# Attention over grouped heads: 24 output buffers instead of 8, stores issued 30 steps behind instead of 14

## The chip, the cores and the metric

The kernel runs on one core of a Trainium2 chip. The metric is the device time of one execution in microseconds (us); the time shown is the median of several runs. A profile is one more execution, taken by the hardware profiler; its span runs from the first to the last instruction on the core. The engines are named as in the profile: PE (matmul; PEld is its weight load), DVE (VectorE), ACT (ScalarE), POOL (GpSimd) and SP (SyncE, which here issues every DMA).

## The reference

Softmax attention with grouped heads: 16 batches, 32 query heads, 8 key/value heads, 16 queries, 2048 keys, head size 128, all bf16.

```python
B, Hq, Hkv, Sq, Sk, D = 16, 32, 8, 16, 2048, 128

def reference(q, k, v):
    rep = Hq // Hkv
    k = jnp.repeat(k, rep, axis=1)
    v = jnp.repeat(v, rep, axis=1)
    scores = jnp.einsum("bhqd,bhkd->bhqk", q, k) * D ** -0.5
    p = _softmax(scores, axis=-1)
    return jnp.einsum("bhqk,bhkd->bhqd", p, v)
```

Four query heads share one key/value head, so a key/value head has 64 query rows. K and V are 67 MB each and are read once; the output is 2.1 MB.

## The kernel before

The work is cut into 64 pairs of key/value heads (`NP = 64`). The two heads of a pair fill 128 partitions with their query rows. For each pair p there is a chain: K is transposed on DVE (`kt`, L351), PE makes the scores (`S`, L300 and L256), DVE scales them, copies them out and finds the maximum (L373), ACT takes the exponential (`exp`, L413), PE transposes the result (`PT`, L312), ACT copies that out (L423), PE multiplies it with V (`PV`, L330 for most pairs, L336 for the others), and the product is scaled and written as bf16 to an output buffer `Osb` (the norm): on ACT (L436 or L440) for pairs 0 to 58, on DVE (L394) for the last `NLATE = 5`. The order of work on PE and ACT is laid down in two lists, `pe_prog` and `act_prog`; PV and norm of a pair come four pairs (`PVLAG`) behind its exponential.

K comes in loads of 2 MB for two pairs, into `NK = 3` buffers; V in loads of 1 MB, one pair each, into `NV = 7` buffers (the last one in two parts, L221); q in eight loads of 256 KB. The output of a pair is a store of 32 KB: 128 rows of 256 bytes.

All of these are issued by SP, on one queue and in the order of one loop over steps t (L238 to L247). A step may have a load of q, then the load of K for pairs t and t+1 (even t), the load of V for pair t-6 (`VLAG`), and the store of pair t-14 (`SLAG`). Each waits first for what it needs:

- `load_k` (L208) for the transposes that free its buffer,
- `load_v` (L216, L221) for the PV that frees its buffer, that of seven pairs before,
- `store` (L236) for the norm of its pair: `sem_nm` from ACT, `sem_nl` from DVE for the last five.

While SP waits, or while an issue does not go through, nothing that stands behind it on SP is issued. After the loop SP waits for the semaphores of all output buffers (L249), and that ends the kernel.

An output buffer is pair p modulo `NO`. Each has a semaphore, `sem_o`, that its store raises by 16 when it has landed. The norm of pair p waits until the store of pair p - `NO` has landed (L432 on ACT from pair `NO` on, L392 on DVE). The PV of the next pair waits for a norm too (`sem_nm`, L322), because most pairs share one accumulator in PSUM.

Of the kernel before, what the change touches and what calls it, by code (L numbers as in the profile page):

```python
# [13 lines left out]
NKT = 2  # L14
NS = 3
NPT = 4
NO = 8
NQ = 2
NSTAGE = 3
VLAG = 6  # L20
PVLAG = 4
SLAG = 14
QLEAD = 7
LASTV = ((0, 12), (12, 16))
NFAST = 8
# [7 lines left out]
def bass_standalone__gqa_softmax__sampling_kernel(  # L33
# [11 lines left out]
    NP = G // 2  # L45
# [24 lines left out]
    PT = [sb(f"PT{i}", [128, J // 2, 128], F32) for i in range(NPT)]  # L70
    Osb = [sb(f"O{i}", [128, 128], BF16) for i in range(NO)]
    nhalf = sb("nhalf", [128, 2, NP], F32)
# [12 lines left out]
    sem_q = [sem(f"sem_q{i}") for i in range(NQ)]  # L85
    sem_o = [sem(f"sem_o{i}") for i in range(NO)]
    sem_kt = sem("sem_kt")
# [91 lines left out]
    with nc.Block() as block:  # L179

        @block.gpsimd
        def _(gp):
            gp.iota(iota_m[:, :, :], [[-8, 4], [-32, 4]], base=0, channel_multiplier=1).then_inc(sem_id, 1)
            gp.iota(iota_t[:, :], [[1, 128]], base=0, channel_multiplier=-1).then_inc(sem_id, 1)
            gp.wait_ge(sem_id, 2)
            gp.tensor_scalar(ident4[:, :], iota_t[:, :], 0.0, None, op0=ALU.is_equal).then_inc(sem_id, 1)
            gp.tensor_scalar(lo_m[:, :, :], iota_m[:, :, :], 0.0, None, op0=ALU.is_ge).then_inc(sem_id, 1)
            gp.tensor_scalar(hi_m[:, :, :], iota_m[:, :, :], 8.0, None, op0=ALU.is_lt).then_inc(sem_id, 1)
            gp.wait_ge(sem_id, 5)
            gp.tensor_tensor(lo_m[:, :, :], lo_m[:, :, :], hi_m[:, :, :], op=ALU.mult).then_inc(sem_id, 1)  # L190
            for x in range(2):
                gp.wait_ge(sem_id, 6 + x)
                a = lo_m[:, :, :] if x == 0 else hi_m[:, :, :]
                w = 2 >> x
                dst = hi_m[:, :, 0:2] if x == 0 else mask[:, :].unsqueeze(2)
                gp.tensor_tensor(dst, a[:, :, 0:w], a[:, :, w:2 * w], op=ALU.add).then_inc(sem_id, 1)
            gp.wait_ge(sem_id, 8)
            for c in range(1, NQC):
                gp.wait_ge(sem_st, last_q[c - 1, 3] + 1)
                lay_q(gp, c)  # L200

        @block.sync
        def _(sp):
            def load_k(n):
                s = n % NK
                if n >= NK:
                    sp.wait_ge(sem_kt, 4 * (n - NK) + 4)
                sp.dma_start(Kn[s][:, :], kf[n]).then_inc(sem_k[s], 16)  # L208

            def load_v(p):  # L210
                s = p % NV
                if p >= NV:
                    sp.wait_ge(sem_pv, p - NV + 1)
                if p < NP - 1:
                    dst = Vb[s][:, :, :, :].rearrange("a g j d -> a g (j d)")
                    sp.dma_start(dst, vf[:, 2 * p:2 * p + 2, :]).then_inc(sem_v[s], 16)  # L216
                    return
                for x, (lo, hi) in enumerate(LASTV):
                    dst = Vb[s][:, :, lo:hi, :].rearrange("a g j d -> a g (j d)")
                    src = vf[:, 2 * p:2 * p + 2, 128 * lo:128 * hi]  # L220
                    sp.dma_start(dst, src).then_inc(sem_vl[x], 16)  # L221

            def load_q(c):
                s = c % NQ
                if c >= NQ:
                    sp.wait_ge(sem_q4, 4 * (c - NQ + 1))
                src = qf[1024 * c:1024 * (c + 1), :].rearrange("(a j) d -> a j d", j=8)
                sp.dma_start(Qn[s][:, :, :], src).then_inc(sem_q[s], 16)

            def store(p):  # L230
                s = p % NO
                if p < NP - NLATE:
                    sp.wait_ge(sem_nm, p + 1)
                else:
                    sp.wait_ge(sem_nl, p - (NP - NLATE) + 1)
                sp.dma_start(of[128 * p:128 * (p + 1), :], Osb[s][:, :]).then_inc(sem_o[s], 16)  # L236

            for t in range(NP + SLAG + 1):  # L238
                for c in range(NQC):
                    if t == max(0, 8 * c - QLEAD):  # L240
                        load_q(c)
                if t < NP and t % 2 == 0:
                    load_k(t // 2)
                if 0 <= t - VLAG < NP:
                    load_v(t - VLAG)
                if 0 <= t - SLAG < NP:
                    store(t - SLAG)  # L247
            for s in range(NO):
                sp.wait_ge(sem_o[s], 16 * (NP // NO))  # L249

        @block.tensor
        def _(pe):
# [15 lines left out]
            for op in pe_prog:  # L268
                if op[0] == "QT":
                    _, c, i, u = op  # L270
                    if i == 0:
                        pe.wait_ge(sem_q4, 4 * (c + 1))
# [6 lines left out]
                    ins.then_inc(sem_st, 1)  # L279
                elif op[0] == "S":  # L280
                    _, n = op
                    pe.wait_ge(sem_kt, 2 * n + 2)
                    if n >= 1:
# [19 lines left out]
                    ins.then_inc(sem_s, 1)  # L303
                elif op[0] == "PT":
                    _, p, h, u = op
                    if h == 0:
                        pe.wait_ge(sem_exp, p + 1)
# [38 lines left out]
        def _(dve):  # L346
# [41 lines left out]
            for p in range(NP - NLATE, NP):  # L388
                if p == NP - 2:
                    recip(NQD - 1)  # L390
                dve.wait_ge(sem_rec, p // 2 + 1)
                dve.wait_ge(sem_o[p % NO], 16 * (p // NO))  # L392
                dve.wait_ge(sem_pv, p + 1)
# [76 lines left out]
```

## Time and profile before

| | |
|---|---|
| median of 3 runs | 342.99 us (342.74 to 343.7) |
| profiled execution, span | 340.7 us |
| DVE busy | 304.8 us (89%) |
| PE busy | 304.3 us (89%) |
| ACT busy | 253.6 us (74%) |
| bytes moved by DMA | 138.87 MB, mean 408 GB/s |

The page lists the DMA issues with the median time from issue to landing:

```profile
Kn<-in_k_dram SPq DMA_DIRECT2D x32, 2048.0 KB, 15.3
Vb<-in_v_dram SPq DMA_DIRECT2D x63, 1024.0 KB, 16.6
out_dram<-O SPq DMA_DIRECT2D x64, 32.0 KB, 16.1
```

The busy times are sums over the whole execution. "Share" of a DMA queue is the time that its packets took, as a part of the span of 16 DMA engines. The time of an issue on SP (SPq) is how long SP was held by it, not how long the transfer took; the time to landing runs from the start of the issue to the last byte.

### The profile page before, as it was taken

The page shows a single profiled execution, that of the slowest core. Times are in us where ns is not written, and L with a number is a line of the kernel's source. Part 1 is how long each engine was busy: PE and PEld are TensorE (multiplying, and loading weights), DVE is VectorE, ACT ScalarE, POOL GpSimd, SP SyncE. Part 2 cuts the span into 40 slices and gives each one's busy share as a digit, 9 for nine tenths or more (in the row PEclk, how much of TensorE's full clock was granted, in tenths as well). Part 3 has the DMA queues.
Part 4 walks back from the last instruction along what each step waited for, and adds up shares of the span by engine and source line. Part 5 has one row for each costly group of instructions (what it writes and reads, how often), then busy time and mean ns, then how long its engine had stood idle before and what let it go on. Part 6 is the DMA issues. An engine that isn't in the chain of part 4 may idle for free.

```text
span 340.7 us, 7084 instructions
## 1 busy us (share of the span) xinstructions
PE 304.3 (89%) x3040; PEld 182.4 (54%) x2528; DVE 304.8 (89%) x457; ACT 253.6 (74%) x390; POOL 81.3 (24%) x40
## 2 busy tenths in 40 slices
PE   3466798999899998999989999999989999899987
PEld 3012355555655664566555556556645665555556
DVE  1879998999989997999989999899979999899952
ACT  3025776789777888778867897778887788678875
POOL 2840007500092004900075000920039000000000
PEclk9759999999999999999999999999999999999999
DMA  7999999999999999999999999999999999999993
GB/s 294 443 415 420 425 415 414 411 419 422 424 423 410 415 419 424 416 420 407 419 426 423 419 405 417 421 428 415 412 418 416 426 418 423 408 419 415 410 407 121
DMA packets 32688, 138.87 MB, mean 408 GB/s; under 512 B 10896, under 2 KB 11152, under 8 KB 28560
## 3 DMA queue, kind: packets, MB, share of 16 engines
q1 hardware_dynamic: 32656, 138.42, 99.5%
q8 instruction: 22, 0.36, 0.4%
q14 instruction: 10, 0.08, 0.1%
HBM read 136.31 MB, written 2.10 MB: 406 GB/s over the span
## 4 chain that ended last, share of the span: by engine, by line
PE 55%; DVE 28%; ACT 9%; issue 5%; DMA 2%; ACTq 0%; SPq 0%; DVEq 0%
PE O_ps L330 17%; DVE Sneg L373 17%; PE S_ps L300 14%; PE S_ps L256 12%; DVE KT L351 11%; PE ST_ps L312 8%; ACT P L413 4%; ACT QT L404 2%; DMA Kn<-in_k_dram 2%; PE ST_ps L278 2%; ACT PT L423 2%; ACT O L436 1%; PE S_ps L336 1%; PE O_ps L336 1%; DVE rrec L359 0%
## 5 line engine op out<-in xcount | busy, mean ns | idle before, releaser
L373 DVE TENSOR_SCALAR_CACHE_REDUCE Sneg<-S_ps 128x1024 f32<-128x1024 f32 x128 | 150.7, 1213 | 19.1 <-PE S_ps L256 18.9
L351 DVE STREAM_TRANSPOSE KT<-Kn 128x1024 f32<-128x1024 f32 x128 | 150.8, 1217 | 3.9 <-DMA Kn<-in_k_dram 3.9
L413 ACT ACTIVATE P<-Sneg,nbias 128x2048 bf16<-128x2048 f32 x64 | 128.2, 2004 | 16.1 <-DVE nbias L381 15.1
L300 PE MATMUL S_ps<-KT,QT 64*128 64x512 bf16 x512 | 103.5, 394 | 24.1 <-DVE Sneg L373 12.8
L174 POOL TENSOR_SCALAR Q<-Qn,mask 128x1024 bf16<-128x1024 bf16 x28 | 79.1, 2843 | 181.1 <-PE ST_ps L278 174.6
L256 PE MATMUL S_ps<-KT,QT 64*128 64x512 bf16 x512 | 103.1, 392 | 0.0
L330 PEld LDWEIGHTS O_ps<-Vb,PT 128*128 128x128 bf16 x672 | 62.4, 98 | 34.7 <-issue 28.0
L330 PE MATMUL O_ps<-Vb,PT 128*128 128x256 bf16 x672 | 80.7, 273 | 0.0
L423 ACT ACTIVATE PT<-ST_ps 128x512 f32<-128x512 f32 x128 | 69.3, 595 | 13.1 <-PE ST_ps L312 12.1
L300 PEld LDWEIGHTS S_ps<-KT,QT 64*128 64x128 bf16 x512 | 27.4, 94 | 93.7 <-issue 72.4
L312 PE MATMUL ST_ps<-ident,P 128*128 128x128 f32 x512 | 67.6, 275 | 4.1 <-ACT P L413 4.1
L436 ACT ACTIVATE O<-O_ps,rrec 64x128 bf16<-64x128 f32 x84 | 30.4, 362 | 46.2 <-PE O_ps L330 45.7
L312 PEld LDWEIGHTS ST_ps<-ident,P 128*128 128x128 f32 x512 | 56.9, 141 | 10.3 <-ACT P L413 7.8
L278 PE MATMUL ST_ps<-ident,Q 128*128 128x128 f32 x128 | 20.4, 291 | 5.2 <-DVE Q L174 5.2
L404 ACT ACTIVATE QT<-ST_ps 128x512 f32<-128x512 f32 x32 | 19.3, 604 | 5.1 <-PE ST_ps L278 5.1
L336 PEld LDWEIGHTS O_ps<-Vb,PT 128*64 128x64 bf16 x576 | 16.7, 110 | 11.5 <-issue 11.5
L336 PE MATMUL O_ps<-Vb,PT 128*64 128x128 bf16 x576 | 19.5, 221 | 0.6 <-ACT O L440 0.6
L278 PEld LDWEIGHTS ST_ps<-ident,Q 128*128 128x128 f32 x128 | 16.4, 152 | 5.2 <-issue 5.2
L413 ACT ACTIVATION_READ_ACCUMULATOR P<-Sneg,nbias 128x1 f32 x64 | 12.2, 191 | 0.0
L373 DVE DVE_READ_ACCUMULATOR Sneg<-S_ps 128x1 f32 x128 | 10.6, 83 | 0.0
L440 ACT ACTIVATE O<-O_ps,rrec 128x128 bf16<-128x128 f32 x17 | 6.0, 351 | 2.2 <-PE O_ps L336 2.2
L381 DVE TENSOR_TENSOR nbias<-nhalf 128x2 f32<-128x2 f32 x32 | 5.1, 160 | 1.1
(19 smaller groups left out, 20.1 us busy)
## 6 DMA issues: line engine op xcount, KB each, us to landing
Kn<-in_k_dram SPq DMA_DIRECT2D x32, 2048.0 KB, 15.3
Vb<-in_v_dram SPq DMA_DIRECT2D x63, 1024.0 KB, 16.6
Qn<-in_q_dram SPq DMA_DIRECT2D x8, 256.0 KB, 13.3
out_dram<-O SPq DMA_DIRECT2D x64, 32.0 KB, 16.1
Vb<-in_v_dram SPq DMA_DIRECT2D x1, 768.0 KB, 12.0
Vb<-in_v_dram SPq DMA_DIRECT2D x1, 256.0 KB, 12.3
```

The source lines that it names most:

```text
L174: eng.tensor_scalar(Q4[:, :, :, r, :].rearrange("p j b x -> p (j b) x"), src, mask[:, r:r + 1], None, op0=ALU.mult,).then_inc(sem_q4, 1)
L256: return pe.add_instruction(mybir.InstMatmult(name=nc.get_next_instruction_name(), engine=mybir.EngineType.PE, ins=[pe.lower_ap(rhs), pe.l ...
L278: ins = pe.transpose(dst[:, 128 * j:128 * (j + 1)], src[:, 4 * x + j, b, :], ident4[:, :])
L300: ins = pe.matmul(s_ap, w, x, start=(acc == 0), stop=(acc == 3))
L312: ins = pe.transpose(dst[:, 128 * t:128 * (t + 1)], P[p % 2][:, 128 * x:128 * (x + 1)], ident4[:, :])
L330: ins = pe.matmul(O_ps[:, 0:256], pt[:, j // 2, j % 2, :], Vb[p % NV][:, :, j, :], start=(j == 0), stop=(j == J - 1),)
L336: ins = pe.matmul(o_ap(p)[64 * g:64 * (g + 1), :], pt[:, j // 2, j % 2, 64 * g:64 * (g + 1)], Vb[p % NV][:, g, j, :], start=(j == 0), stop ...
L351: dve.transpose(KT[n % NKT][:, :].rearrange("p (t b g e a) -> p e g t b a", t=J // 4, b=2, g=4, e=2)[:, e], Kn[Q % NK][:, :].bitcast(F32). ...
L373: dve.tensor_scalar(Sneg[p % NS][:, 1024 * x:1024 * (x + 1)].rearrange("p (t a m) -> p t a m", t=4, m=8), S_ps[:, 1024 * y:1024 * (y + 1)] ...
L413: act.activation(P[p % 2][:, :].bitcast(BF16), Sneg[p % NS][:, :], ACT.Exp, bias=nbias[:, p:p + 1], scale=-1.0, accum_out=rowsum[:, p:p + ...
L423: act.activation(PT[p % NPT][:, 4 * h:4 * (h + 1), :].rearrange("p t q -> p (t q)"), stage_ap(u), ACT.Copy,).then_inc(sem_ev, 1)
L436: ins = act.activation(Osb[p % NO][rows, :], O_ps[rows, 128 * g:128 * (g + 1)], ACT.Copy, scale=rrec[rows, p:p + 1])
```

## The change

Two constants change, and the wait that ends the kernel is written so that it fits a number of buffers that does not divide 64: with 24 buffers, buffers 0 to 15 are used three times and 16 to 23 twice.

```diff
-NO = 8
+NO = 24
 NQ = 2
 NSTAGE = 3
 VLAG = 6
 PVLAG = 4
-SLAG = 14
+SLAG = 30
...
             for s in range(NO):
-                sp.wait_ge(sem_o[s], 16 * (NP // NO))
+                sp.wait_ge(sem_o[s], 16 * ((NP - s + NO - 1) // NO))
```

The first store is issued at step 30 instead of step 14; the loop (`range(NP + SLAG + 1)`) runs 16 steps longer. The output buffers take 6 KB of each partition instead of 2 KB. Everything else, the order of the loads and the programs of the other engines among it, stays as it was.

## The prediction

> **What bounds the kernel now.** I read first the page's shares and its chain of waits, then the waits of SP's queue, then the tail: SP's timeline and the issues with their landings, one by one, and the DMA share by microsecond.
>
> ```profile
> span 340.7 us, 7084 instructions
> PE 304.3 (89%) x3040; PEld 182.4 (54%) x2528; DVE 304.8 (89%) x457; ACT 253.6 (74%) x390; POOL 81.3 (24%) x40
> q1 hardware_dynamic: 32656, 138.42, 99.5%
> PE 55%; DVE 28%; ACT 9%; issue 5%; DMA 2%; ACTq 0%; SPq 0%; DVEq 0%
> L351 DVE STREAM_TRANSPOSE KT<-Kn 128x1024 f32<-128x1024 f32 x128 | 150.8, 1217 | 3.9 <-DMA Kn<-in_k_dram 3.9
> ```
>
> Two things are full at once: the transfers (99.5%) and the pair DVE/PE (89% each). The chain that sets the end is compute; DMA has 2% of it, all at the start, and the transposes of K waited for a transfer once, 3.9 us. So loads arrive in time, and stores are no part of the path except the very last one. What sits between is SP, which issues every transfer from one queue:
>
> ```profile
> 315.52 2.58 SPq L236 DMA_DIRECT2D out_dram<-O  x1
> 320.42 1.27 SPq L216 DMA_DIRECT2D Vb<-in_v_dram  x1
> 324.03 0.38 SPq L221 DMA_DIRECT2D Vb<-in_v_dram  x1
> 324.45 1.25 SPq L221 DMA_DIRECT2D Vb<-in_v_dram  x1
> 325.75 0.48 SPq L236 DMA_DIRECT2D out_dram<-O  x1
> 326.27 2.56 SPq L236 DMA_DIRECT2D out_dram<-O  x1
> 329.17 0.89 SPq L236 DMA_DIRECT2D out_dram<-O  x1
> 331.21 0.33 SPq L236 DMA_DIRECT2D out_dram<-O  x1
> 338.81 0.33 SPq L236 DMA_DIRECT2D out_dram<-O  x1
> ```
>
> Columns: start, duration. An issue takes 0.33 us after a pause and 0.43 to 0.48 right behind another one, but 1 to 3 us where the queue in front of the DMA engines has no room. That the long ones are a full queue is my reading; the durations shrink as the queue empties (0.33 from 331 us on). The last nine stores (pairs 55 to 63) follow the last V load; the last is issued at 338.81, when its data are ready, and ends the kernel.
>
> ```profile
> Vb<-in_v_dram SPq DMA_DIRECT2D x1, 256.0 KB, 12.3
> out_dram<-O SPq DMA_DIRECT2D x1, 32.0 KB, 11.2
> out_dram<-O SPq DMA_DIRECT2D x1, 32.0 KB, 10.9
> out_dram<-O SPq DMA_DIRECT2D x1, 32.0 KB, 1.5
> 337.00:338.00 1.00, 1.00 (x43) 1.00 (x40) 0.35 (x1) 0.10 (x1) 0.00 (x0) 1.00 0.02 3
> SPq L221 <- PE O_ps L336: 0.9, 1, 0.9
> ```
>
> The issues are those at 324.45, 325.75, 326.27 and 338.81; the last number is us to landing. So V of pair 63 has landed at 324.45 + 12.3 = 336.8, the stores behind it at 336.95 and 337.15 (0.2 us apart), and the last store at 340.3, which leaves 0.4 us to the span's end. From 337 us the DMA engines are idle (share 0.02, the next to last number). V of pair 63 is issued when PV of pair 56 frees its buffer (the 0.9 us wait of L221), so its issue time is given by compute.
>
> **The change, part by part.** *The order.* At step t SP issues K, V(t-6), store(t-30). V(63) is step 69: 25 stores (39 to 63) now come behind it, 9 before. Sixteen more stores, all with data long ready, stand ahead of stores 55 to 63 in SP's queue. Nothing but stores is behind them; only the end of the kernel waits for them.
>
> *The buffers.* Norm(p) waits for store(p-24), issued right behind V(p); before it was store(p-8) in the same place (24-30 = 8-14). PV(p) has waited for V(p) by then. The last one, norm(63) on DVE at 338.43 us, needs store 39, which lands 0.2 us behind V(63), by 337.0 at the latest: 1.4 us of cover. Pairs 8 to 23 lose a wait that cost nothing (norm on ACT shows only PV as what ended its idle time). I take 0.
>
> *Less traffic ahead of the loads.* Sixteen stores leave the stretch before V(63). Loads move up, but the chain waits for none of them after the start, and the stores begin at 55 us: gain 0. It is 0 at the other end too as long as the 3.9 us of waiting for K lie before 55 us, as they do. How far V(63) moves up matters for the next part. By bytes a store is 32 KB at the 418 GB/s of the full stretches, 0.08 us; by the landings at the end it is 0.2 us. Between loads the first is nearer: two V loads issued at 36.15 and 36.63 land 2.5 us apart without a store between them, those at 315.04 and 318.15 land 2.6 us apart with one. I take 0.1: 1.6 us earlier (1.3 to 3.2), so V(63) lands at 335.2 (333.6 to 335.5).
>
> *SP at the end.* The queue holds a limited number of packets per DMA engine. A store is 8 data packets and 1 completion for each of 16 engines, a V load 16 and 1 (the page's 10,896 packets under 512 B are 64 x 128 + 169 issues x 16). When the blocked store of 326.27 went through at 328.83, the V load of 315.04 had just landed (13.8 us). Still in the queue were stores of 315.52, 319.39, 321.73, 325.75 and 326.27 and the V loads of 318.15, 320.42 and the two parts of pair 63: 5 x 9 + 2 x 17 + 34 = 113 packets. The same count at the other ends of blocked issues from 325 us on gives 105 to 130. So at most about 113/9 = 12.5 stores can be queued when V(63) lands (11.7 to 14.4), however early SP comes to them. Unblocked it would come to 17 or more: V(63) is issued by 324.9, and (335.2 - 324.9)/0.52 is 20. The queue decides.
>
> Then 24 - 12.5 = 11.5 stores are still to be issued ahead of store 63. From there the engines take 0.2 us for one, SP 0.48 and a gap of 0.04: the two stores at 325.75 and 326.27 start 0.52 us apart (the other end: 0.33 + 0.04 = 0.37, a price that shows only after a pause; I take the row of two neighbours). 11.5 x 0.52 = 6.0: store 63 is issued at 335.2 + 6.0 = 341.2 in place of 338.81, **+2.4 us**. Corners: 333.6 + 9.6 x 0.37 = 337.2, in time, +0; 335.5 + 12.3 x 0.52 = 341.9, +3.1. Nothing is queued ahead of it then, so its landing stays 1.5 us.
>
> *The waits at the end.* SP waits for 24 semaphores instead of 8. Store 63 is buffer 15; eight waits come after it, none did before. The 0.4 us between the last landing and the span's end hold everything SP does there today, so eight waits cost 0 to 0.5; I take **+0.3**.
>
> Sum: 340.7 + 2.4 + 0.3 = 343.4 for the profiled execution; the runs' median, 342.99, lies 2.3 above its span, so 342.99 + 2.7 = **345.7**, 0.8% slower.
>
> One sentence of the Trainium skill speaks against this: "DMA: Bandwidth & Descriptors", section "Issuing engines are not separate DMA queues", holds the sequencer's time to issue a transfer to be "usually small relative to the DMA itself". Here the row is the other way round, 0.52 us of issue against 0.2 us of transfer, and what the rule would give is the first rival.
>
> **Rivals.** *A: the end stays where it is (not slower).* The mechanism: once V(63) has landed, the transfers and not SP set the pace. 24 stores behind 335.2 at 0.2 us are through at 340.0, store 63 at 340.3 as now: 342.99 to 343.3 with the waits. For it: the 0.2 us between landings, the idle engines from 337 us, and a V(63) that could land as early as 333.6. It also comes out at these times if SP issues at 0.37 us and the queue takes 14 stores. Against it: neighbours at 0.43 to 0.48 us wherever the queue is free. It decides where (24 - n) x spacing is under 338.8 less V(63)'s landing, 3.6 us: n of 17 at 0.52, or 0.31 us a store at 12.5. This includes halfway cases up to 344.0.
>
> *B: the queue has less room.* In the stretch with K loads in it, issues were blocked with fewer packets queued: the store of 297.51 went through at 304.06 with some 90. If that is the limit, 10 stores are queued at 335.2 less what other work takes, 14 to 15 are left, 14.5 x 0.52 = 7.5: 342.7, +3.9 and the waits 0.3: 347.2. For it: that row. Against it: the counts from 325 us on, where only 4 KB and smaller packets are queued.
>
> *C: faster.* Loads that come 1.6 us earlier let compute move up by as much, 341.4, if a wait for V or K hides in PE's or DVE's idle time at the end. Against it: none of the idle time after the start is put down to a load, and rising landing times (13 us early, 20 us near 280 us) have not yet reached the chain.
>
> **How the numbers follow.** Forecast as worked, 344.2 to 346.7: 0.48. A, 342.7 to 344.0: 0.27. B, 346.7 to 348: 0.18. C: 0.04; others 0.03. Predicted is the likeliest, 345.7. The range 343.0 to 347.6 holds the forecast, most of A and most of B. A measurement of this kernel tells about 0.3%, 1.0 us, from no change: faster C, 0.04; same the part of A below 344.0, 0.20 (the rest of A lies at its edge); slower 0.76.
>
> **What would show it.** SP's timeline after the last V load: 25 stores without a pause, the first dozen at about 1.4 us each while V drains (9 packets at 0.16 us), then some twelve at 0.52, and store 63 issued at about 341 instead of 338.8, with DVE's last norm still at 338.4 to 338.8. The chain of waits should end on SP. V(63) should land near 335. If the last stores start 0.37 us or less apart, or SP waits for DVE at the last store, A is right; if the norm itself moves, my view of the buffers or of the loads is wrong. Loads that arrive later than before would refute the sum at its root.

## The result and the profile after

The changed kernel takes 346.58 us (346.31 to 346.81) beside 342.87 us for the kernel before in the same comparison: ratio 1.0117, 95% interval 1.0098 to 1.0135, so 3.4 to 4.6 us slower. The forecast was 345.7 in a range of 343.0 to 347.6. A second comparison of the same two kernels (below) gave 1.0088 (1.0067 to 1.0110), 3.0 us; the sum of the prediction, +2.7, stands under both medians.

The page of the changed kernel: the span, the busy times, the queue, the chain, and the row of K's transposes.

```profile
span 344.8 us, 7092 instructions
PE 305.7 (89%) x3040; PEld 183.3 (53%) x2528; DVE 304.8 (88%) x457; ACT 253.9 (74%) x390; POOL 81.4 (24%) x40
q1 hardware_dynamic: 32656, 138.42, 98.6%
PE 54%; DVE 28%; ACT 9%; issue 5%; DMA 2%; SPq 0%; ACTq 0%; DVEq 0%
L351 DVE STREAM_TRANSPOSE KT<-Kn 128x1024 f32<-128x1024 f32 x128 | 150.8, 1217 | 4.8 <-DMA Kn<-in_k_dram 4.8
```

No byte more is moved, and DVE and ACT are busy as long as before. PE is busy 1.4 us longer; in the traces of the other kernels below it is busy for 303.0 to 305.5 us whether they are slower or not, so this says nothing of the change. The chain looks like that of before, with nothing on SP: it ends on DVE's last norm and leaves out what SP does behind it. The loss has to be read on SP and at the end. SP's timeline and DVE's (start, duration):

```profile
325.23 0.38 SPq L221 DMA_DIRECT2D Vb<-in_v_dram  x1
325.65 0.47 SPq L221 DMA_DIRECT2D Vb<-in_v_dram  x1
326.17 16.50 SPq L236 DMA_DIRECT2D out_dram<-O  x25
334.26 1.27 SPq L236 DMA_DIRECT2D out_dram<-O  x1
337.95 1.39 SPq L236 DMA_DIRECT2D out_dram<-O  x1
342.24 0.43 SPq L236 DMA_DIRECT2D out_dram<-O  x1
340.51 0.35 DVE L394 TENSOR_SCALAR O<-S_ps,rrec 128x128 bf16<-128x128 f32 x1 [0.54 <-PE S_ps L336]
```

The landings of the V issue at 325.65 and of the store at 342.24 (us from the issue, last number), and then the windows of one microsecond at the end (the DMA share is the number before the last):

```profile
Vb<-in_v_dram SPq DMA_DIRECT2D x1, 256.0 KB, 10.5
out_dram<-O SPq DMA_DIRECT2D x1, 32.0 KB, 1.6
```

```profile
341.00:342.00 1.00, 0.00 (x0) 0.00 (x0) 0.00 (x0) 0.00 (x0) 0.00 (x0) 1.00 0.31 67
342.00:343.00 1.00, 0.00 (x0) 0.00 (x0) 0.00 (x0) 0.00 (x0) 0.00 (x0) 1.00 0.30 66
```

The last norm is done at 340.9, its store is issued at 342.2: SP is 1.4 us late, where before it stood waiting for that norm. From the first issue of the last V load to the issue of store 63 it takes 342.24 - 325.23 = 17.0 us, before 338.81 - 324.03 = 14.8. From 341 to 343 us every compute engine is idle and the DMA engines are busy for 0.3 of the time: the core waits for SP to hand over small stores one after another. From the last landing (342.24 + 1.6 = 343.8) to the end of the span it is 0.96 us by the unrounded times, before 0.47.

The difference of the two spans, 4.1 us: 1.2 from an issue of the last V load that is that much later (K came 0.8 us later at the start, and DVE's transposes are 1.2 us behind from 30 us on: one pair starts at 29.81 instead of 28.63 us), 2.2 in the stretch to store 63, 0.1 in its landing, 0.5 in the waits at the end. The first of these was suspect, since nothing at the start differs.

### The profile page after: what moved, and what is told of

It is laid out like the page before. It is cut to its first block, busy times and chain, and to the rows that moved or that the text cites. A ratio compares the mean times of both kernels' runs of the same rounds, so it can differ in the third digit from the quotient of the medians.

```text
span 344.8 us, 7092 instructions
## 1 busy us (share of the span) xinstructions
PE 305.7 (89%) x3040; PEld 183.3 (53%) x2528; DVE 304.8 (88%) x457; ACT 253.9 (74%) x390; POOL 81.4 (24%) x40
## 3 DMA queue, kind: packets, MB, share of 16 engines
q1 hardware_dynamic: 32656, 138.42, 98.6%
## 4 chain that ended last, share of the span: by engine, by line
PE 54%; DVE 28%; ACT 9%; issue 5%; DMA 2%; SPq 0%; ACTq 0%; DVEq 0%
PE O_ps L330 17%; DVE Sneg L373 17%; PE S_ps L300 14%; PE S_ps L256 12%; DVE KT L351 11%; PE ST_ps L312 8%; ACT P L413 4%; DMA Kn<-in_k_dram 2%; ACT QT L404 2%; PE ST_ps L278 2%; ACT PT L423 2%; ACT O L436 1%; PE S_ps L336 1%; PE O_ps L336 1%; DVE rrec L359 0%
## 5 line engine op out<-in xcount | busy, mean ns | idle before, releaser
L312 PE MATMUL ST_ps<-ident,P 128*128 128x128 f32 x512 | 68.4, 277 | 4.2 <-ACT P L413 4.2
L312 PEld LDWEIGHTS ST_ps<-ident,P 128*128 128x128 f32 x512 | 57.6, 142 | 10.6 <-ACT P L413 8.5
## 6 DMA issues: line engine op xcount, KB each, us to landing
Qn<-in_q_dram SPq DMA_DIRECT2D x8, 256.0 KB, 12.7
```

What stands on the lines that cost most here:

```text
L312: ins = pe.transpose(dst[:, 128 * t:128 * (t + 1)], P[p % 2][:, 128 * x:128 * (x + 1)], ident4[:, :])
```

## The experiments

"The tail" is SP's time from the first issue of the last V load to the issue of store 63. All ratios are to the kernel before on the same chip.

| kernel | stores behind the last V load | ratio, 95% interval | tail, us |
|---|---|---|---|
| before | 9 | 1 | 14.8 |
| 24 buffers alone | 9 | 1.0017 (1.0002 to 1.0031) | 14.8 |
| 16 buffers, 22 steps | 17 | 0.9997 (0.9986 to 1.0007) | 14.8 |
| 20 buffers, 26 steps | 21 | 1.0034 (1.0019 to 1.0049) | 15.9 |
| the change | 25 | 1.0117 (1.0098 to 1.0135) | 17.0 |
| the change, again | 25 | 1.0088 (1.0067 to 1.0110) | 17.7 |
| the change, one wait at the end | 25 | 1.0088 (1.0066 to 1.0111) | 17.0 |
| 32 buffers, 38 steps | 33 | 1.0174 (1.0159 to 1.0189) | 20.6 |
| 16 tiny loads in place of 16 stores | 9 and 16 | 1.0081 (1.0060 to 1.0101) | 16.9 |
| 16 stores in two DMAs | 11 | 1.0038 (1.0024 to 1.0052) | 15.0 |
| 16 stores on GpSimd | 9, and 16 there | 1.0005 (0.9990 to 1.0021) | 14.8 |
| catching up ahead of the last V load | 9 | 1.0011 (0.9986 to 1.0035) | 12.9 |

**Buffers alone.**

```diff
-SLAG = 30
+SLAG = 14
```

> 24 output buffers and the 24 waits at the end, but the stores 14 steps behind, as before the change: 9 stores behind the last V load. My theory (SP cannot issue the 16 extra stores in time): the whole loss but the waits is gone. Eight waits of 0.06 us come after the last landing, so +0.5 us: 343.4, ratio 1.001 to 1.002. Rival, that the buffers themselves cost (other addresses, more semaphores, the later start of the first scores that the changed kernel's trace shows): it stays slower by 1.5 us or more, ratio 1.004 to 1.011.

Measured: 343.22 us, ratio 1.0017, +0.6 us. The buffers, their addresses and the 24 waits together cost what the waits were put at, within an interval of 0.1 to 1.1 us; the first K load landed at the same time as in the trace of before (8.9 us). So the later stores carry the rest.

**Dose: 16, 32 and then 20 buffers.** The distance between `NO` and `SLAG` stays at 6, so that the number of stores behind the last V load varies, and besides it only the number of buffers and of waits at the end.

```diff
-NO = 24
-SLAG = 30
+NO = 16   # 20, 32
+SLAG = 22 # 26, 38
```

> 16 buffers, stores 22 steps behind: 17 stores behind the last V load, half of the step of the change. My theory has a threshold: about 13 to 15 stores are issued by the time that the last V load lands, the rest at 0.47 us each is done before the last norm, so the time is that of before plus 0.25 us of waits: 343.1, ratio 1.000 to 1.003. Rival, that each store moved behind the loads costs its transfer (3.7 us / 16 = 0.23 us each, in proportion): +1.9 us, ratio 1.005 to 1.006.

> 32 buffers, stores 38 steps behind: 33 stores behind the last V load. My theory: past the threshold every further store costs SP's issue, 0.47 us, so 8 x 0.47 = 3.8 us and 0.25 us of waits over the changed kernel: about +7.7 us against before, ratio 1.021 to 1.024. Rival, in proportion to the stores moved at 0.23 us each: +5.6 us, ratio 1.015 to 1.017.

> 20 buffers, stores 26 steps behind: 21 stores behind the last V load, between the 17 that cost nothing and the 25 of the change. In the trace with 17, SP had 0.8 us to spare at the last store. Four stores more cost 4 x 0.47 us of issue less 4 x 0.1 us by which the last V load lands earlier, 1.5 us; less the spare 0.8, plus 0.1 of waits: +0.8 us against before, ratio 1.001 to 1.004. In proportion to the stores moved (3.7 us x 12/16) it would be +2.8 us, ratio 1.007 to 1.009.

Measured: 0.9997, 1.0174 and 1.0034. Eight more stores behind the loads are free, twelve cost 1.2 us, sixteen 3.0 to 4.0, twenty-four 6.1. A price in proportion is excluded by the first and the third; there is a threshold. What SP had to spare shows it: the row of its waits for DVE's last norms, in the kernels with 9, 17 and 21 stores behind the load. With 25 there is no such row.

```profile
SPq L236 <- DVE O L394: 5.8, 5, 1.7
```

```profile
SPq L236 <- DVE O L394: 2.0, 3, 1.0
```

```profile
SPq L236 <- DVE O L394: 0.3, 1, 0.3
```

The total (first number) has to be read beside SP's timeline, for the row also counts a norm that is done while SP is held in an issue. The 5.8 us are five pauses between issues. Of the 2.0 us, 1.0 falls into an issue that was held from 335.38 to 336.96 us; two pauses are left, 0.4 and 0.5 us, ahead of the last two stores. The 0.3 us lie inside this issue, and the next starts at 339.20 us, without a pause:

```profile
338.73 0.43 SPq L236 DMA_DIRECT2D out_dram<-O  x1
```

So 17 stores leave SP 1.0 us to spare, and 21 nothing.

With 32 buffers my expectation was too high, 7.7 against 6.1 us. For the eight stores past the change I had put 8 x 0.47 = 3.8 us; the tail grew by 3.6 us over the first trace of the change and by 2.9 over the second, because the holds that the next experiments show are uneven (4.5 us in this trace, 4.7 and 5.4 in those of the change). And I had added 0.25 us of waits, where the stretch from the last landing to the end is 0.47 us again instead of 0.96: store 63 uses the last of the 32 buffers, and its wait is the last one.

**The change once more.**

> The changed kernel once more, for a second trace. In its first trace the first scores came 1.2 us later than in the trace of before, PE paused 0.65 us in the middle of PV of pair 61, and SP was held 1.4 us at a store (338.0 us) while an instruction load of 16 KB ran. If the later start is chance, it is gone or different here. If the pause and the hold belong to the change, both come again at the same stores; if they are chance, the time of the tail from the first issue of the last V load to the last store's issue falls from 17.0 to about 16.1 us. Time as before in either case within 1 us: ratio 1.009 to 1.014.

Measured: 346.0 us, ratio 1.0088; the profiled execution is the slowest of these, 346.95 us. K's first load landed at 8.9 us and PE did not pause in PV of pair 61: K's late landing and the pause of the first trace were chance. Yet the last V load was again issued later than before, at 324.83 instead of 324.03 us. This does not come from the stores: DVE is 0.8 us behind the trace of before from 29 us on (a transpose at 29.42 instead of 28.63 us), still so at its last transposes (321.76 and 320.97), and the first store of before is issued at 55.6 us. The holds came again, but at other stores (the 8th and 13th instead of the 12th and 18th), and the tail is not shorter but 17.7 us. Here are the stores of SP's timeline around them, and the DMA queues in the windows 331.9 to 333.0 and 335.5 to 336.9:

```profile
332.00 1.42 SPq L236 DMA_DIRECT2D out_dram<-O  x1
335.37 1.94 SPq L236 DMA_DIRECT2D out_dram<-O  x1
337.36 0.43 SPq L236 DMA_DIRECT2D out_dram<-O  x1
```

```profile
q1 hardware_dynamic: 189, 0.25, 61.8%
q8 instruction: 1, 0.02, 6.1%
...
q1 hardware_dynamic: 540, 0.12, 40.7%
q8 instruction: 1, 0.02, 6.2%
```

In each window one instruction load of 16 KB occupies one DMA engine (6.1% of 16 engines in 1.1 us is 1.1 us, 6.2% in 1.4 us is 1.4), and the store whose issue falls into it holds SP for 1.4 and 1.9 us, about 1.0 and 1.5 more than its neighbours.

**One wait at the end.** The last store of each buffer raises one common semaphore.

```diff
-                sp.dma_start(...).then_inc(sem_o[s], 16)
+                sp.dma_start(...).then_inc(sem_o[s] if p < NP - NO else sem_fin, 16)
...
-            for s in range(NO):
-                sp.wait_ge(sem_o[s], 16 * ((NP - s + NO - 1) // NO))
+            sp.wait_ge(sem_fin, 16 * NO)
```

> The changed kernel with one semaphore for the last store of every buffer, so that the end waits once instead of 24 times. My theory: from the last landing to the end of the span 0.4 us as before the change in place of 0.9, so -0.5 us against the changed kernel, ratio 1.008 to 1.012. Rival, that the waits run while the last store is on its way and cost nothing: no change, 1.010 to 1.014, and 0.9 us stay in the trace.

Measured: 346.0 us, ratio 1.0088 (1.0066 to 1.0111), the same as the change in the same comparison. In the trace the time from the last landing to the end is 0.40 us in place of 0.96, but the runs do not show the half microsecond. It stays a reading of the trace.

**Issues without bytes.** To 24 buffers with the old lag, 16 tiny loads are added, which fill a tile that nothing reads.

```diff
-SLAG = 30
+SLAG = 14
...
+                if t == NP - 1 + VLAG:
+                    for i in range(16):
+                        sp.dma_start(tiny[:, 32 * i:32 * (i + 1)], qf[16 * i:16 * (i + 1), 0:32]).then_inc(sem_ty, 16)
```

> 24 buffers, stores 14 steps behind (the first experiment), and 16 tiny extra loads of 1 KB into a tile nobody reads, issued between the last V load and the nine stores: as many issues as the change puts there, but 2 packets per DMA engine in place of 9. Theory A, a full queue and the issue time together: 32 packets do not fill the queue, the holds behind the last V load shrink, 24 issues at 0.47 us and one or two holds by instruction loads reach 338 to 339 us, just when the last norm is done: 0.5 to 1.0 us over before, ratio 1.0015 to 1.004. Theory B, the issue time alone: as the changed kernel, ratio 1.009 to 1.013. Theory C, the transfers alone: the extra ones weigh nothing, ratio 1.000 to 1.002.

Measured: 345.73 us, ratio 1.0081: +2.9 us, as much as the change run beside it. SP's timeline behind the last V load:

```profile
325.70 11.76 SPq L251 DMA_DIRECT2D tiny<-in_q_dram  x16
337.50 4.22 SPq L239 DMA_DIRECT2D out_dram<-O  x9
```

Sixteen issues of 1 KB hold SP for 11.8 us. Theory C, that only transfers count, is out. Theory A, mine, is out in its size: 2 packets per engine in place of 9 buy hardly anything. What A left small are the holds: 0.46 x 16 = 7.4 us are issue time, the other 4.3 are one hold at the still full queue (1.6 us) and three more, two of them during the instruction loads (1.2 and 1.3 us).

**Bytes without issues.** The 16 stores go out in two DMAs, at the place of stores 39 and 48.

```diff
-    Osb = [sb(f"O{i}", [128, 128], BF16) for i in range(NO)]
+    Oall = sb("Oall", [128, NO, 128], BF16)
+    Osb = [Oall[:, i, :] for i in range(NO)]
...
+                dst = of[128 * a:128 * b, :].rearrange("(n a) d -> a n d", a=128)
+                sp.dma_start(dst, Oall[:, a % NO:a % NO + b - a, :]).then_inc(sem_mg[i], 16)
```

> The changed kernel, but the 16 stores that moved behind the last V load (pairs 39 to 54) go out in two DMAs (nine and seven pairs, one tile of SBUF), with the same bytes in the same 256-byte rows, at the place of stores 39 and 48; then the nine others one by one. My theory: 14 issues fewer on SP, 14 x 0.47 = 6.6 us, more than the loss, so store 63 goes out as soon as it is there: about +0.5 us against before, ratio 1.000 to 1.003. Rival, that the transfers of 16 x 4096 packets behind the loads are what takes the time: no change against the changed kernel, ratio 1.010 to 1.013.

Measured: 344.13 us, ratio 1.0038, +1.3 us; neither the expected 0.5 nor the rival's 4. (The 16 stores are 16 x 128 = 2,048 packets of 256 bytes, not the 16 x 4096 of the expectation.) SP's timeline:

```profile
325.44 6.97 SPq L245 DMA_DIRECT2D out_dram<-Oall  x2
332.45 7.46 SPq L239 DMA_DIRECT2D out_dram<-Oall  x9
```

The second large DMA and the store behind it had to wait for room (6.45 and 2.98 us), so that SP came free at 335.4 and issued store 63 at 339.48, 0.2 us after its norm. The queue's limit is real, but only a store of many packets feels it to this extent.

**The same stores from another engine.** GpSimd issues the 16 stores from the moment that the last V load is issued, one by one as SP did. GpSimd has nothing else to do by then.

```diff
+            gp.wait_ge(sem_pv, NP - NV)
+            for p in range(39, 55):
+                gp.wait_ge(sem_nm, p + 1)
+                gp.dma_start(of[128 * p:128 * (p + 1), :], Osb[p % NO][:, :]).then_inc(sem_po[p - 39], 16)
...
-                if 0 <= t - SLAG < NP:
+                if 0 <= t - SLAG < NP and t - SLAG not in range(39, 55):
```

> The changed kernel, but the 16 stores of pairs 39 to 54 are issued by GpSimd, from the moment that PV of pair 56 frees the last V load, so that the same bytes still go behind or beside the last V load and SP has only the nine others to issue. My theory (SP's time): SP waits for the norm again at the last store, and the tail is as before unless GpSimd itself ends later; what one issue costs there no run has shown, up to 0.85 us each it is hidden (16 x 0.85 = 13.6 us from 325 us). Sixteen semaphores more at the end add 0.5 us, buffers and waits 0.5: +0.5 to +1.1 us, ratio 1.001 to 1.004. Rival, the transfers: as the changed kernel, 1.009 to 1.012.

Measured: 343.23 us, ratio 1.0005 (0.9990 to 1.0021). The timeline of POOL and of SP's stores, and the row of SP's wait for the last norms:

```profile
324.10 8.70 POOL L206 DMA_DIRECT2D out_dram<-O  x16 [60.84 <-PE O_ps L345]
324.75 14.17 SPq L242 DMA_DIRECT2D out_dram<-O  x9
```

```profile
SPq L242 <- DVE O L406: 5.9, 5, 1.7
q0 software_dynamic: 512, 0.53, 0.5%
```

The bytes of the change still move in the tail, and the loss is gone; SP has its 5.9 us to spare again. The packets are not the same: on GpSimd's queue, q0 in the last line, the 0.53 MB went in 256 packets of 2 KB and 256 small ones, where SP's queue lost 2,304 (32,656 in the change, 30,352 here), and they landed about 5 us after their issue, ahead of the V load that SP issued beside them (12.7 us). So this run alone would leave cheaper transfers as a rival. The tiny loads close that gap: hardly any bytes, as many issues on SP, and the whole loss. Together they settle the cause: SP's own time for 16 issues more in the tail, with the holds among them.

**Catching up ahead of the last V load.** Thirty steps behind up to step 52, then two stores a step, so that again nine stand behind it.

```diff
+                if t < 53:
+                    ps = [t - SLAG]
+                elif t < 69:
+                    ps = [23 + 2 * (t - 53), 24 + 2 * (t - 53)]
+                else:
+                    ps = [t - 14]
```

> The changed kernel up to step 52, with stores 30 steps behind; from step 53 to 68 two stores a step, so that again nine stand behind the last V load. My theory, only the place behind the last V load costs: +0.5 us as in the first experiment, ratio 1.000 to 1.003. Rival, late stores cost wherever they are, or 16 more stores among the last sixteen steps hold up the loads, of which the last K load had 0.6 us to spare before: ratio 1.005 or more, and DVE or PE waits for a load in the trace.

Measured: 343.56 us, ratio 1.0011 (0.9986 to 1.0035). Late stores cost nothing that the runs show in the middle of the kernel, nor does the double rate ahead of the last loads; no compute engine waited for a load but for K and q at the start. The last V load itself was issued 2.6 us later than before, counted from the landing of the first K load, and landed 0.7 us later; nothing waited for it. Only the place behind the last V load is dear.

## Why the prediction was right, and where not

*What bounds the kernel, and the order.* Right. 25 stores without a pause stand behind the last V load, DVE's norm of pair 63 waits for PE and not for a store, and the end is SP's. Two signs were wrong. The chain of waits does not end on SP: it counts what SP waits for, not the time in which SP issues, and follows the end back to the last norm. And the last norm did move: it starts at 340.51 us in the first trace and at 339.23 in the second, where the prediction had 338.4 to 338.8. That was to speak against its view of the buffers or the loads, but the delay is that of the start (1.2 and 0.8 us) and, in the first trace, 0.9 us more behind PE's pause of 0.65.

*The buffers.* Right: no wait for a store shows in the traces, and the kernel with buffers alone (+0.6 us, of which the waits are put at 0.5) leaves nothing clear of noise.

*Less traffic ahead of the loads.* The direction was right, no gain and none in any run. The size, 1.6 us by which V of pair 63 lands earlier, was somewhat large: from the landing of the first K load it is 327.9 us before, 327.4 with 8 stores moved, 327.2 with 12, between 325.9 and 327.1 in four traces with 16, and 326.5 with 24. That is 0.05 to 0.12 us for a store; the middle, 1.4 us for 16, is nearer to the end of my bounds that goes by bytes, 0.08.

*SP at the end.* The price was nearly right and half of its reason wrong. The step that failed is "The queue decides", with the 113 packets that let 12.5 stores through before the last V load lands, against 20 without the limit. 14 and 13 stores had been issued by then in the two traces, which looks like the forecast but came about otherwise. The sign that went with a full queue, about 1.4 us for each of the first dozen, failed (and did not fit the forecast itself: a dozen would take 17 us, not the 10.3 that it had until V lands): they took 0.78 us each in the first trace. Holds that I read as a full queue come in the first seven stores only, 2.8 us in all; the last of these holds ended at 332.3 and 332.0 us, some 4 us before V landed. And the tiny loads, which hardly fill the queue, went little faster: the fifteenth was being issued at the same point. What fills the tail is issue time, 24 x 0.475 = 11.4 us (0.43 and a gap of 0.045; I had 0.52), and holds of 4.7 and 5.4 us in the two traces: the 2.8 us at the full queue, and the rest mostly at the two instruction loads, which the prediction did not have at all. That the sum came out at +2.2 us (first trace) for the predicted +2.4 is in part luck: a limit that was made to last until V lands, and an issue price that was a little high, stood in for holds that were not seen. In the second trace it is +3.0.

*The waits at the end.* The term was under-sized in the traces of the change, 0.5 us for 0.3; the runs cannot tell whether it counts.

*The rivals.* A, that transfers set the pace behind the last V load, fell with the tiny loads and with GpSimd. The rule of the Trainium skill that went with it ("DMA: Bandwidth & Descriptors", section "Issuing engines are not separate DMA queues", the issue usually small against the transfer) does not hold for stores of 32 KB here: 0.47 us of issue against 0.15 to 0.2 us between landings of queued stores (a store by itself takes 1.5 us to land). The same section also says that issuing from several engines saves the sequencer's time and nothing else; the run on GpSimd agrees in so far as that saving is the whole loss, though the stores also went in other packets there. B, a tighter queue, is near in its time (347.2) but not in its mechanism. C, that earlier loads speed compute up, left no trace in any run.

The medians stand 0.9 and 0.3 us above the forecast. In the traces the terms that came out larger than forecast are the stretch to store 63 (second trace) and the waits: with 0.1 us for the landing they make 2.8 and 3.5 us, near the 3.7 and 3.2 us between the medians. The later start, 1.2 and 0.8 us of the two profiled spans, lies ahead of all stores and is no part of the change.

## What to carry to other kernels

A transfer that is put off is issued later too, and the engine that issues it may have less time there: count the issues behind the last load, times the interval of two neighbouring issues, and set this against the time that the issuing engine still waits in that stretch. Here SP waited 7.3 us in all behind the last V load (5.8 for DVE's norms, 1.5 for ACT's); 8 issues fitted, 16 with their holds did not. The count leaves out the holds: by it 12 issues (5.7 us) would have fitted too, but they left no pause and cost 1.2 us. The chain of waits does not show such a limit; the pauses between the issues of the issuing engine do, by disappearing.

## What had not been expected

In a dense row of issues, the issue on SP that falls into an instruction load of 16 KB is held until shortly after that load, even where few packets are queued: in the first trace of the change the store at 337.95 us took 1.39 us while the two ahead of it took 0.43, and in that of the change run again the hold of 1.94 us at 335.37 ended 0.4 us after the load did. Each trace with a dense row of issues in the tail shows such holds at one or both of its instruction loads there (0.8 to 1.9 us an issue). In the trace of before, stores issued after a pause, at 331.21 and 335.87 us, went through in 0.33 us although such loads were running. That the load is the cause was not tried.

GpSimd issued its 16 stores in 8.7 us, 0.54 us each, with no long hold among them, though SP was held for 2.9 us at one store in the same stretch, and an instruction load of 16 KB ran in it (330.9 to 331.9 us).
